# A new head and a new order for a fused attention and MLP kernel on one Trainium2 core

The kernel normalises 2048 rows, runs a sliding dilated attention and a GELU MLP on them, and adds both to the input. The change touches the first 20 us (what is loaded first, which engine takes which statistics, how the first chunk is projected) and then the order of everything after.

## The chip, the cores and the metric

One Trainium2 chip (trn2), one of its cores. The metric is the device time of one execution in microseconds, as a median of several runs; lower is better. The span in a profile (first to last instruction) is some 2.1 us shorter than the time of the same run. "Clock" is the granted clock of TensorE, 1.0 for full speed.

## The reference, cut to what matters

```python
# x: 1 x 2048 x 640 (bf16); 32 heads of 20; window W = 8, dilation 2; F = 1536
xn = layernorm(x)                                  # no gain, no bias
q, k, v = split_heads(xn @ wqkv)
# row s of head h looks at rows s, s-2, ..., s-14
attn = softmax(where(mask, q . k[s - 2*w], -1e9) * 20**-0.5)
A = (sum over w of attn[w] * v[s - 2*w]) @ wo
B = gelu(xn @ w1 + b1) @ w2 + b2
return x + A + B
```

## The kernel before

The rows are in 4 chunks of 512, each of 4 blocks of 128. Per chunk the rows are normalised, transposed, projected to q, k, v (TensorE), multiplied shifted against each other (VectorE), summed per head by TensorE into logits, turned into weights, spread over the head's 20 columns by four DMA issues of 256 KB (`ax`), multiplied with v (VectorE) and projected with `wo`, while TensorE and ScalarE run the MLP beside them.

The order on TensorE, VectorE, ScalarE and SyncE's queue is not written by hand. A planner at build time simulates the kernel: each piece has an engine, an estimated duration, a rank, needs, buffers and an earliest landing of its data. Whenever an engine is free, the ready piece of lowest rank comes next. The emitted order is then final; each engine takes its pieces strictly in this order. GpSimd has no order in the plan: it issues what it is given when its needs are met. Transfers too are entered with fixed durations or landing times.

Of the kernel before, what the change touches and what calls it, by code (L numbers as in the profile page):

```python
# [18 lines left out]
class Plan:  # L19
# [111 lines left out]
EPS = 1e-5  # L131
MASKED = -1e9
MW = 16
LASTB = S // P - 1
WARM = 44

GROUPS = (((0, 0, 4),), ((1, 0, 4),), ((0, 4, 5), (1, 4, 5)), ((2, 0, 4),), ((2, 4, 5),))
# [4 lines left out]
    "av1": 36.4, "av2": 74, "f12": 4.1, "f13": 69.4, "gj1": 19.4, "gj2": -19.4, "o02": -8.9, "o10": 15.3,  # L142
    "o12": -3.3, "o13": -11.3, "o20": 117, "o31": 57.5, "o33": 85.2, "ot0": 20, "pj22": -106.4, "pj31": -13.1,
    "qk1": -4.8, "qk2": 4.4, "st2": 164.2, "st3": 219.3, "xn0": -14.7,
# [3 lines left out]
def make_plan(fns, offsets=RANK):  # L148
# [10 lines left out]

    def done(n, which):  # L160
        if n:
            return [f"pc{n}{which}{to}" for to in range(KT)]
        return [f"gc{bl}{g}" for bl in range(BPC) for g, parts in enumerate(GROUPS) if which in [p[0] for p in parts]]

    pl.add("b1", VE, 0.1, -90, [], f("b1"), after=21.0)
    for n in range(NCH):
# [6 lines left out]
        for bl in range(BPC):  # L173
            land = (4.0, 4.0, 9.6, 9.6)[bl] if n == 0 else (0.0, 13.3, 17.1, 17.1)[n]
            r = -40 if n else -99
            pl.add(f"st{n}{bl}a", VE, 0.5, r, [], f("st", n, bl, 0), after=land)
            pl.add(f"st{n}{bl}", VE, 0.62, r, [f"st{n}{bl}a"] + ([f"rc{n}{bl - 1}"] if n == 0 and bl else []), f("st", n, bl, 1))
            if n == 0:
                pl.add(f"rs{n}{bl}", SE, 0.35, -99, [f"st{n}{bl}"], f("sqrt", n, bl, bl + 1), table="sqrt")
                pl.add(f"rc{n}{bl}", VE, 0.17, -99, [f"rs{n}{bl}"], f("rstd", n, bl, bl + 1))  # L180
# [3 lines left out]
        for bl in range(BPC):  # L184
            xn, tp = ("xn", n, bl), ("acc", "tp", n, bl)
            if n > 0:
                pl.add(f"xn{n}{bl}", SE, 0.81, early + -4.0, [f"rc{n}"], f("xn", n, bl), [xn])
                pl.add(f"tc{n}{bl}", DQ, 4.0 if n > 1 else 2.7, early - 3.0, [f"xn{n}{bl}"], f("td", n, bl), [xn, xnT], 21.5)
                continue

            for i, (a, b) in enumerate(((0, 2), (2, KT)) if bl == 0 else ((0, KT),)):
                u = "a" if b < KT else ""
                us = (b - a) / KT
                pl.add(f"xn{n}{bl}{u}", VE, 0.06 + 0.36 * us, -99, [f"rc{n}{bl}"], f("xn", n, bl, a, b), [xn])
                pl.add(f"tp{n}{bl}{u}", PE, (0.54 if bl == 0 else 0.3) * us, -99, [f"xn{n}{bl}{u}"], f("tp", n, bl, a, b), [xn, tp])
                pl.add(f"tc{n}{bl}{u}", SE, 0.16 + 0.49 * us, -99, [f"tp{n}{bl}{u}"], f("tc", n, bl, a, b), [tp, xnT])
        if n == 1:
            pl.add("ld", DQ, 9.2, -1000, [f"tc1{bl}" for bl in range(BPC)], f("ld"))
# [3 lines left out]
        if n == 0:  # L202
            for bl in range(BPC):
                for g, parts in enumerate(GROUPS):
                    ps, last = ("acc", "g", bl, g), max(p[0] for p in parts)
                    tos = sum(p[2] - p[1] for p in parts)
                    land = (6.4, 8.7, 11.8)[last]
                    r = -50 + (last == 2)
                    need, cut = [f"tc0{bl}"], 0
                    if bl == 0 and g == 0:  # L210
                        cut = 2
                        need.append(pl.add("ga00", PE, 0.112 * tos, r, ["tc00a"], f("gj", bl, g, 0, cut), [xnT, ps], land))
                    pl.add(f"gj{bl}{g}", PE, 0.056 * (KT - cut) * tos, r, need, f("gj", bl, g, cut, KT), [xnT, ps], land)
                    pl.add(f"gc{bl}{g}", SE, (0.27, 0.54, 0, 0.54)[tos - 1], -50, [f"gj{bl}{g}"], f("gc", bl, g), [ps] + [(q, k, v)[p[0]] for p in parts])
        for which, buf in enumerate((q, k, v)):
            for to in range(KT if n else 0):
                ps = ("acc", "p", n, which, to)
                r = early + (0 if which < 2 else 20.0)
                pl.add(f"pj{n}{which}{to}", PE, 1.08, r, [f"tc{n}{bl}" for bl in range(BPC)], f("pj", n, which, to), [xnT, ps])
                pl.add(f"pc{n}{which}{to}", SE, 0.52, early + 0.0, [f"pj{n}{which}{to}"], f("pc", n, which, to), [ps, buf])  # L220
            if which:
                need = done(n - 1, which) if n else []
                bufs = [buf] + ([("k" if which == 1 else "v", n - 1)] if n else [])
                pl.add(f"pad{n}{which}", SE, 0.26, early if n else -50, need, f("pad", n, which), bufs)
# [37 lines left out]
        for ft in range(FT):  # L262
            ps = ("acc", "h", n, ft)
            pl.add(f"f1{n}{ft}", PE, 1.08, base + 10.0 + 1.0 * ft, [f"tc{n}{bl}" for bl in range(BPC)], f("f1", n, ft), [xnT, ps], 22.5)
            pl.add(f"ge{n}{ft}", SE, 0.6, base + 0.0, [f"f1{n}{ft}", "b1"], f("ge", n, ft), [ps, hTs[ft]], table="gelu")
# [24 lines left out]
def kernel(  # L290
# [50 lines left out]
    nc.sync.dma_start(x_sb[:, 0, :], x_nb[:, 0, :])  # L341
    nc.scalar.dma_start(x_sb[:, 1, :], x_nb[:, 1, :])
    for s in range(3):
        nc.sync.dma_start(wqkv[s][:], wqkv_v[:, :, s * D : (s + 1) * D])
        if s == 1:
            nc.sync.dma_start(x_sb[:, 2:BPC, :], x_nb[:, 2:BPC, :])
    nc.sync.dma_start(b1_rt[0:FT, :], B_b1.rearrange("(t p) -> t p", p=P))
    for cs in (slice(BPC, 2 * BPC), slice(2 * BPC, NCH * BPC)):
        nc.sync.dma_start(x_sb[:, cs, :], x_nb[:, cs, :])
    nc.sync.dma_start_transpose(b1_t[:], b1_rt[:])  # L350
    nc.sync.dma_start(w1_sb[:], B_w1.rearrange("(t p) n -> p t n", p=P))
# [8 lines left out]
    zeros = consts.tile([P, P], BF16, name="zeros")  # L360
    nc.vector.memset(zeros[:], 0.0)  # L361
# [5 lines left out]
    nc.scalar.activation(warm[:], eps_t[:], ACT.Sqrt)  # L367
# [15 lines left out]
    std = consts.tile([P, NCH * BPC], F32, name="std")  # L383
    rstd = consts.tile([P, NCH * BPC], F32, name="rstd")
# [10 lines left out]
    def do_st(n, bl, i):  # L395
# [3 lines left out]
        if i:  # L399
            nc.vector.bn_aggr(mv[:, b, :], stats[:])  # L400

# [31 lines left out]
    def do_tp(n, bl, a, b):  # L433
        xn = tiles["xn", n, bl]
        tp = get(("tp", n, bl), lambda: psA.tile([P, 2 * CH], BF16, tag="acc", name="tp"))
        for t in range(a, b):
            nc.tensor.transpose(tp[:, t * P : (t + 1) * P], xn[:, t * P : (t + 1) * P], ident[:])  # L437

    def do_tc(n, bl, a, b):
        xnT = get(("xnT", n), lambda: xtp.tile([P, KT, CH], BF16, tag="xnT", name="xnT"))  # L440
        nc.scalar.copy(  # L441
            xnT[:, a:b, bl * P : (bl + 1) * P],
            tiles["tp", n, bl][:, a * P : b * P].rearrange("p (t m) -> p t m", t=b - a),
        )

    def do_td(n, bl):
        xnT = get(("xnT", n), lambda: xtp.tile([P, KT, CH], BF16, tag="xnT", name="xnT"))
        nc.sync.dma_start_transpose(xnT[:, :, bl * P : (bl + 1) * P], tiles["xn", n, bl][:])
# [43 lines left out]
    def do_gj(bl, g, a, b):  # L492
        cs = slice(bl * P, (bl + 1) * P)
        ps = get(("gps", bl, g), lambda: psA.tile([P, BPC, P], F32, tag="acc", name="gps"))
        slots = [(which, to) for which, lo, hi in GROUPS[g] for to in range(lo, hi)]
        pairs = [(i, ti) for i in range(len(slots)) for ti in range(a, b)]
        if b - a < KT:
            pairs.sort(key=lambda p: p[1])
        for i, ti in pairs:
            which, to = slots[i]  # L500
            nc.tensor.matmul(  # L501
                ps[:, i, :],
                lhsT=wqkv_p[which][:, ti, to, :],
                rhs=tiles["xnT", 0][:, ti, cs],
                start=(ti == 0 and (i == 0 or b == KT and a == 0)),
                stop=(ti == KT - 1 and (i == len(slots) - 1 or b == KT and a == 0)),
                skip_group_check=True,
            )

    def do_gc(bl, g):  # L510
        i = 0
        for which, a, b in GROUPS[g]:
            off = (0 if which == 0 else PAD) + bl * P
            nc.scalar.copy(qkv_tile(0, which)[:, a:b, off : off + P], tiles["gps", bl, g][:, i : i + b - a, :])
            i += b - a
# [205 lines left out]
    with tc.manual_schedule(engines=engines):  # L721

        idle = psL.tile([P, W, P], F32, tag="L", name="idle")
        for _ in range(WARM):
            nc.tensor.matmul(idle[:, 0, :], lhsT=zeros[:], rhs=zeros[:], start=True, stop=True)  # L725
# [32 lines left out]
```

## Time and profile before

| | before |
|---|---|
| time, median of 3 runs | 214.81 us (214.52 to 214.85) |
| span of the profiled run, clock | 212.4 us, 1.0 |
| busy: TensorE, VectorE, ScalarE | 97%, 82%, 52% |
| TensorE's first projection | 7.03 us |
| TensorE ends, span ends | 209.65, 212.4 us |

### The profile page before, as it was taken

The numbers are of one execution on the slowest core, as the hardware profiler recorded it, in microseconds if no ns is written. First come the engines' busy times: TensorE is split into PE (matmuls) and PEld (weight loads), VectorE is DVE, ScalarE is ACT, GpSimd is POOL, SyncE is SP. The second block draws the span as 40 slices with busy tenths as digits, with TensorE's granted clock in tenths as the row PEclk, the third lists the DMA queues.
The fourth block names the chain that finished last, engine by engine and source line by source line (L and its number), as shares of the span: only waits on it lengthen the run. The fifth ranks groups of instructions, "written<-read, shape, count | busy, mean of one in ns | idle before, by whom it ended". The sixth has DMA issues, their size and how long they took to land.

```text
span 212.4 us, 3961 instructions
## 1 busy us (share of the span) xinstructions
PE 206.9 (97%) x1670; PEld 121.7 (57%) x1693; DVE 174.4 (82%) x178; ACT 109.5 (52%) x193; POOL 19.7 (9%) x37
## 2 busy tenths in 40 slices
PE   8999999999999999999999999999999999999994
PEld 8799845655545555555555555455555455555552
DVE  3579999759999997599996999999999999972001
ACT  3568997798574654931353883503752511341120
POOL 2000000000020024101100010101110011101130
PEclk9999999999999999999999999999999999999999
DMA  6999528916829199993120027202114611122214
GB/s 216 365 362 376 93 50 275 322 24 132 206 64 163 37 287 196 197 195 89 15 30 0 0 31 200 31 3 31 14 21 48 180 19 22 27 29 31 34 16 76
DMA packets 23465, 23.95 MB, mean 113 GB/s; under 512 B 9112, under 2 KB 20632, under 8 KB 23448
## 3 DMA queue, kind: packets, MB, share of 16 engines
q1 hardware_dynamic: 17864, 16.49, 28.3%
q0 software_dynamic: 4144, 4.92, 17.2%
q10 hardware_dynamic: 1440, 2.29, 3.9%
q8 instruction: 13, 0.21, 0.4%
q14 instruction: 4, 0.03, 0.1%
HBM read 10.00 MB, written 7.54 MB: 83 GB/s over the span
## 4 chain that ended last, share of the span: by engine, by line
PE 97%; issue 1%; DVE 0%; ACT 0%
PE lo L684 27%; PE hps L653 24%; PE pps L484 23%; PE gps L501 8%; PE hi L686 8%; PE L L557 4%; PE idle L725 2%; PE tp L437 1%; ACT xnT L441 0%; DVE osb L714 0%; DVE zeros L361 0%
## 5 line engine op out<-in xcount | busy, mean ns | idle before, releaser
L653 PE MATMUL hps<-xnT,w_sb 128*128 128x512 bf16 x235 | 54.1, 379 | 0.3
L684 PE MATMUL lo<-w_sb,hT 128*128 128x512 bf16 x183 | 51.8, 379 | 0.0
L631 DVE TENSOR_TENSOR pv<-vT,ax 128x2560 bf16<-128x2560 bf16 x32 | 45.9, 1484 | 1.7 <-PE L L557 1.7
L535 DVE TENSOR_TENSOR prod<-qT,kT 128x2560 bf16<-128x2560 bf16 x32 | 45.4, 1484 | 0.0
L686 PE MATMUL hi<-w_sb,hT 128*128 128x128 bf16 x192 | 40.3, 219 | 0.6 <-issue 0.2
L664 ACT ACTIVATE hT<-hps,b1T 128x512 bf16<-128x512 f32 x48 | 31.6, 687 | 17.0 <-PE hps L653 13.3
L653 PEld LDWEIGHTS <-w_sb 128*128 128x128 bf16 x240 | 23.0, 98 | 26.7
L640 DVE TENSOR_TENSOR pv<-pv 128x5120 bf16<-128x5120 bf16 x12 | 33.9, 2825 | 0.4
L684 PEld LDWEIGHTS <-hT 128*128 128x128 bf16 x192 | 18.7, 98 | 22.8 <-issue 0.6
L691 ACT CAST osb<-lo 128x512 bf16<-128x512 f32 x15 | 8.8, 585 | 44.0 <-issue 28.0
L697 POOL DMA_DIRECT2D out_dram<-osb x15 | 12.9, 863 | 110.5 <-ACT osb L692 110.5
L684 PE MATMUL lo<-wo,oT 128*128 128x512 bf16 x79 | 23.0, 379 | 0.0
L686 PEld LDWEIGHTS <-hT 128*128 128x128 bf16 x192 | 18.4, 98 | 1.5
L398 DVE BATCH_NORM_STATS2 stats<-x_sb 128x6 f32<-128x320 bf16 x32 | 14.0, 469 | 5.1 <-DMA x_sb<-in_A_x_dram 5.1
L484 PE MATMUL pps<-xnT,wq_sb 128*128 128x512 bf16 x71 | 16.9, 380 | 0.2
L484 PE MATMUL pps<-xnT,wv_sb 128*128 128x512 bf16 x73 | 16.9, 379 | 0.1
L686 PE MATMUL hi<-wo,oT 128*128 128x128 bf16 x80 | 16.9, 219 | 0.1
L484 PE MATMUL pps<-xnT,wk_sb 128*128 128x512 bf16 x73 | 16.8, 379 | 0.1
L705 DVE TENSOR_TENSOR osb<-lo,x_sb 128x512 bf16<-128x512 f32 x1 | 0.7, 692 | 16.1 <-PE lo L684 16.1
L520 ACT CAST qT<-pps 128x512 bf16<-128x512 f32 x15 | 8.8, 585 | 9.2 <-PE pps L484 9.2
L684 PEld LDWEIGHTS <-oT 128*128 128x128 bf16 x80 | 7.8, 98 | 9.4
L484 PEld LDWEIGHTS <-wk_sb 128*128 128x128 bf16 x75 | 8.7, 118 | 7.3 <-issue 0.2
(62 smaller groups left out, 205.9 us busy)
## 6 DMA issues: line engine op xcount, KB each, us to landing
w_sb<-in_B_w_dram SPq DMA_DIRECT2D x2, 1920.0 KB, 9.2
out_dram<-osb POOLq DMA_DIRECT2D x15, 160.0 KB, 3.4
ax<-attn SPq DMA_DIRECT2D x8, 256.0 KB, 5.4
ax<-attn ACTq DMA_DIRECT2D x8, 256.0 KB, 5.6
out_dram<-x_sb SPq DMA_DIRECT2D x3, 640.0 KB, 4.3
out_dram<-b2bc POOLq DMA_DIRECT2D x3, 640.0 KB, 8.2
x_sb<-in_A_x_dram SPq DMA_DIRECT2D x1, 1280.0 KB, 13.3
wq_sb<-in_A_wqkv_dram SPq DMA_DIRECT2D x1, 800.0 KB, 4.8
```

The costliest lines, as they stand in the source:

```text
L398: nc.vector.bn_stats(stats[:, i, :], x_sb[:, b, i * (D // 2) : (i + 1) * (D // 2)])
L484: nc.tensor.matmul(ps[:], lhsT=wqkv_p[which][:, ti, to, :], rhs=xnT[:, ti, :], start=(ti == 0), stop=(ti == KT - 1),)
L501: nc.tensor.matmul(ps[:, i, :], lhsT=wqkv_p[which][:, ti, to, :], rhs=tiles["xnT", 0][:, ti, cs], start=(ti == 0 and (i == 0 or b == KT an ...
L520: nc.scalar.copy(dest[:, to, off : off + CH], tiles["pps", n, which, to][:])
L535: nc.vector.tensor_tensor(out=prod[:, i, :, :], in0=qkv_tile(n, 0)[:], in1=qkv_tile(n, 1)[:, :, off : off + CH], op=ALU.mult,)
L631: nc.vector.tensor_tensor(out=pv[:, i, :, :].rearrange("p t (j c) -> p t j c", j=BPC), in0=qkv_tile(n, 2)[:, :, off : off + CH].rearrange( ...
L640: nc.vector.tensor_tensor(out=ta[:], in0=ta[:], in1=tb[:], op=ALU.add)
L653: nc.tensor.matmul(ps[:], lhsT=w1_sb[:, ti, ft * P : (ft + 1) * P], rhs=tiles["xnT", n][:, ti, :], start=(ti == 0), stop=(ti == KT - 1),)
L664: nc.scalar.activation(hT[:], tiles["hps", n, ft][:], ACT.Gelu_apprx_tanh, bias=b1T[:, ft : ft + 1], scale=1.0)
L684: nc.tensor.matmul(lo[:], lhsT=lhs, rhs=rhs[:, 0:CH], start=first, stop=last)
L686: nc.tensor.matmul(hi[:, 0 : D - CH], lhsT=lhs, rhs=rhs[:, CH:D], start=first, stop=last)
L697: nc.gpsimd.dma_start(rows, tiles["osb", n, bl][:], accum_op=ALU.add)
```

## The change

Its intent: TensorE is the bound, and it idles only in the head, so bring useful work forward there and save some matmuls' overhead. Block 0 is loaded first and alone, q's weights come in two parts, block 2 and block 3 apart. Block 0's transposes get PSUM tiles of their own, so that the first copy needn't wait for all five. Block 1's mean and variance are taken by ScalarE from accumulated sums. k and v of chunk 0, and q of its blocks 2 and 3, are projected for two blocks at a time. The new plan has other ranks and landing times, hence another order everywhere.

```diff
-WARM = 44
+WARM = 40
 RANK = {
-    "av1": 36.4, "av2": 74, "f12": 4.1, "f13": 69.4, ...
+    "ad02": 84.2, "av1": 114.8, "f11": 43.4, "f12": 139.3, "f13": 100, ...
-            land = (4.0, 4.0, 9.6, 9.6)[bl] if n == 0 else (0.0, 13.3, 17.1, 17.1)[n]
+            land = (3.1, 3.6, 6.1, 8.7)[bl] if n == 0 else (0.0, 12.9, 21.8, 21.8)[n]
+                pl.add("sm", SE, 0.75, -99, [], f("sum1"), after=land)      # block 1 on ScalarE
...                                                          # nm, me, sq likewise
-    nc.sync.dma_start(x_sb[:, 0, :], x_nb[:, 0, :])
-    nc.scalar.dma_start(x_sb[:, 1, :], x_nb[:, 1, :])
-    for s in range(3): ...                                  # q, k, blocks 2 and 3, v
+    load_x(0, 1)
+    load_x(1, 2)                                            # now SyncE's queue
+    load_w(0, 0, 2)
+    load_w(0, 2, KT)
+    load_x(2, 3)
+    load_w(1)
+    load_x(3, BPC)
+    load_w(2)
...
+    load_x(BPC, 2 * BPC)
+    for c in range(2): ...                                  # w1 in two halves
+    load_x(2 * BPC, NCH * BPC)                              # chunks 2 and 3 now behind w1
+    def do_sum1():
+        nc.scalar.activation(trash()[:], x_sb[:, 1, :], ACT.Identity, accum_out=acc1[:])
...
+        pool, tag = (psO, own) if own else (psA, "acc")     # own PSUM tiles for block 0
+        tp = pool.tile([P, 2 * CH], BF16, tag=tag, name="tp")
...
+    def do_gp(which, pair, a, b):                           # 256 columns: two blocks
+                nc.tensor.matmul(ps[:, to - a, :], lhsT=wqkv_p[which][:, ti, to, :],
+                    rhs=tiles["xnT", 0][:, ti, pair * 2 * P : (pair + 1) * 2 * P], ...)
```

## The prediction

> **What bounds the kernel now.** I read four views in this order: the page's busy table with its chain that ended last, the waits of TensorE, the timeline of the first 9 us, and TensorE's timeline afterwards. From the page:
>
> ```profile
> PE 206.9 (97%) x1670; PEld 121.7 (57%) x1693; DVE 174.4 (82%) x178; ACT 109.5 (52%) x193; POOL 19.7 (9%) x37
> PE 97%; issue 1%; DVE 0%; ACT 0%
> ```
>
> TensorE is busy for 97% of the span and carries 97% of the chain that ended last. VectorE, at 82%, is second and is not on the chain. The 97% includes warm-up, so I ask what TensorE waited for. The waits, TensorE only:
>
> ```profile
> PE idle L725 <- DVE zeros L361: 1.0, 1, 1.0
> PE gps L501 <- ACT xnT L441: 0.5, 1, 0.5
> PE hi L686 <- issue: 0.2, 1, 0.2
> ```
>
> There are only two named waits in the whole run, both in the first 7.03 us. Everything this change can win must come from there, or from the matmuls themselves. The timeline of the head (start, duration, engine and operation):
>
> ```profile
> 0.99 4.87 PE L725 MATMUL idle<-zeros 128*128 128x128 bf16 x44 [0.99 <-DVE zeros L361]
> ...
> 3.71 0.89 DVE L398 BATCH_NORM_STATS2 stats<-x_sb 128x6 f32<-128x320 bf16 x2 [2.77 <-DMA x_sb<-in_A_x_dram]
> ...
> 4.87 0.30 ACT L404 ACTIVATE std<-mv,eps_t 128x1 f32<-128x1 f32 x1 [2.18 <-DVE mv L400]
> 5.20 0.16 DVE L408 RECIPROCAL rstd<-std 128x1 f32<-128x1 f32 x1
> 5.40 0.63 DVE L424 TENSOR_SCALAR xn<-x_sb,mv,rstd 128x256 bf16<-128x256 bf16 x2
> ...
> 5.80 0.77 PE L437 MATMUL tp<-ident,xn 128*128 128x128 bf16 x5
> ...
> 6.61 0.75 ACT L441 COPY xnT<-tp 128x256 bf16<-128x256 bf16 x2 [1.44 <-PE tp L437]
> ...
> 7.03 1.28 PE L501 MATMUL gps<-xnT,wq_sb 128*128 128x128 bf16 x20 [0.46 <-ACT xnT L441]
> ```
>
> 44 matmuls that only warm the array fill the time until the first block of x is there. The first useful projection begins at 7.03. The copy of transposed parts 0 and 1 begins only at 6.61, after all five transposes: both halves share a PSUM tile. TensorE's rates afterwards:
>
> ```profile
> 8.74 4.00 PE gps L501 x70
> 16.37 8.65 PE gps L501 x155
> 25.30 8.37 PE hps L653 x38
> ```
>
> These are lines of the chain. 128-column matmuls come every 55.8 ns (8.65/155), and 512-column ones every 0.216 us (eight tiles of five take 8.64 us from 24.86 to 33.50). A pair of 512 and 128 columns takes 0.272 us (12 pairs in 3.26 us).
>
> **A tally from 7.03.** Projection of chunk 0: 300 x 0.0558 = 16.7. Transposes of blocks 1 to 3: 15 x 0.0558 = 0.8. First layer of the MLP: 240 x 0.216 = 51.8. Projections of chunks 1 to 3: 225 x 0.216 = 48.6. Logits: 2.30 + 6 x 1.21 = 9.6. Outputs: 272 x 0.272 = 73.9. Sum 201.5. The final matmul's stream ends about 209.5 (end at 209.65, less the 0.16 by which one modelled matmul exceeds its spacing). So 209.5 - 7.03 = 202.5, and all later stalls together are about 1.0 us. The total time (214.81) is 2.4 us more than the span (212.4).
>
> **What the Trainium skill says.**
> 1. "TensorE: Matmul & The Clock Gate", section "Back-to-back issue gap": an isolated gap of N/2.4 + 2.5 ns when warm, and about 81 ns at N = 128 in a stream that also loads weights. The trace agrees with the first (55.8 ns and 216 ns) and not with the 81 ns.
> 2. The same page, section "Part 1: The HAM clock gate": the array starts at half rate and is released after about 3.4 us of activity, in a free-running window. The trace agrees: 44 warm-up matmuls in about 4.7 us (107 ns each), and 55.8 ns from 7.03.
> 3. "DMA: Bandwidth & Descriptors", section "Anatomy of one DMA": about 2.0 us fixed plus bytes/436e3. For 160 KB alone that is 2.4 us. The trace has 2.9 and 3.1 us for the two blocks sent together: compatible.
> 4. "PSUM — Partial Sum Buffer", section "Engine vs sequencer instructions": the queues of ScalarE and VectorE are strictly first in, first out, and matmuls start in program order. So one late input holds back all behind it. In the trace ScalarE's idle 1.44 us before 6.61 fits that.
>
> **The change part by part.**
>
> *Block 0 first.* In the trace both blocks were issued at 0.74/0.75, block 0 in 2.9 us (landing about 3.65). Alone at first, it saves the half of 320 KB that is not its own: 160 KB at 365 GB/s (page, GB/s row) is 0.45 us. I expect landing near 3.25, block 1 near 3.7.
>
> *Block 1's statistics on ScalarE.* It adds two passes over 640 columns (normalising that shape costs 0.935 us in the trace) and one small one (0.30). VectorE loses two BN_STATS (0.44 each) and one aggregate (0.21), which were behind block 0 anyway. But the sum of block 1 stands before block 0's square root on ScalarE: 3.7 + 0.93 = 4.63, whereas block 0's statistics are ready at 3.25 + 1.13 = 4.38 (3.71 to 4.84 before). So the root starts 4.63 instead of 4.87: of 0.45 us won by loading, 0.24 is left.
>
> *Own PSUM tiles, copy on VectorE.* Normalising starts 0.24 earlier, at 5.16; the second half ends 5.79; the first two transposes, 0.4 us after normalising starts, end about 5.95; VectorE then copies (0.37, taken from the ScalarE row) until 6.35. First projection at about 6.4 instead of 7.03: 0.6 us.
>
> *The rest of the head.* ScalarE: small pass to 5.2, squares to 6.1, root to 6.4, copy of parts 2 to 4 to 6.9. TensorE: 10 matmuls from 6.4, 5 more at 6.95, block 1's transposes about 7.25, 10 more to 8.1, block 1's 25 to about 9.5, first k tiles (10 of 256 columns) to 10.6. The built order then has block 2's transposes, whose square root group stands behind **block 3's statistics** on VectorE. Block 3 lands after the same 2.3 MB as blocks 2 and 3 now (9.54), say 9.3. Statistics 1.13, reciprocal and normalising about 0.5: transposes at 10.95, a stall of about 0.3. Useful work before it: 50 x 0.0558 + 5 x 0.0558 + 10 x 0.1092 = 4.16, so TensorE is as if it had run without a gap from 10.95 - 4.16 = 6.8. Against 7.03: **0.25 us**. If block 3 lands at 8.7, as the changed plan assumes, TensorE itself is the limit, the effective start is about 6.4, and this is 0.6.
>
> *Block pairs.* 250 matmuls of 128 columns become 125 of 256. Interpolating the two rates, 256 columns take 55.8 + 128 x (216 - 55.8)/384 = 109.2 ns. Saved: 125 x (111.6 - 109.2) = **0.3 us**. Fewer ScalarE copies are off the path.
>
> *Warm-up on the constant of ones, 40.* Starts about 0.25 earlier, ends near 5.05; the transposes come near 5.55. Off the path.
>
> *New order.* q and k of chunk 0 are ready about 19.7 instead of 23, since most of v is put off; VectorE starts its products 3 us earlier. I walked VectorE's and TensorE's new order with the durations above: the logit pieces of TensorE at 79.5, 95.3, 110.9 find products ready at 77.5, 94.0, 109.5. No new stall, but only 1.3 to 2 us to spare. Old stalls of 1.0 us may fall by a few tenths.
>
> Sum: 0.25 to 0.6, plus 0.3, plus 0 to 0.3: 0.55 to 1.2, taken as **0.9 us**: 213.9.
>
> **Rivals.**
> (a) *The saved head is taken by the next landing.* TensorE waits for block 3 or for k and v weights: bytes before them are the same as now (k and v landed 8.6 and 11.7). For: DMA is full (365 GB/s) until 20 us. Against: transposes are placed between other work. Then 214.3 to 214.8.
> (b) *VectorE becomes the bound in the middle.* For: margins of 1.3 us in a hand walk; all residual and bias writes now stand in the queue ahead of the first spread of attention weights, and could delay it. Against: its start 3 us earlier. It would cost 0.5 to 2 us: 214.5 to 216.
> (c) *Cold clock.* Fewer warm-up matmuls and small gaps near 5 to 6.4 us leave the array at half rate longer: 51 ns for each of perhaps 15 to 50 matmuls, 0.8 to 2.5 us. Against: before too had gaps of 0.4 us and was warm at 7.03.
> (d) *All goes as the plan wants*: 1.2 to 1.5 us, 213.3 to 213.6.
>
> **Range and chances.** (d) and the main line carry most: 213.1 to 214.9 should hold it 8 times in 10. A gain of 2% (4.3 us) is impossible from a head in which useful work starts at 7.03 and data at 3.7; a loss of 2% needs (b) or (c) at their worst.
>
> **What would show it.** First projection near 6.4 and, on the chain, no stall over 0.5 us after block 2's transposes; pair matmuls 109 ns apart; the first products of VectorE near 20; TensorE's waits after 11 us still under 1 us. It is wrong if block 0 lands no earlier, if ScalarE's sum does not delay the root, if early projections run at 107 ns, or if TensorE waits for logits' products after 70 us.

## More of the kernel before

```python
for name, n in (("acc", 4), ..., ("osb", 2), ("xn", 2), ...):   # buffers
    pl.pool(name, n)
...
for bl in range(BPC):       # chunks 1 to 3: ScalarE normalises, a DMA transposes
    pl.add(f"xn{n}{bl}", SE, 0.81, early - 4.0, [f"rc{n}"], f("xn", n, bl), [xn])
    pl.add(f"tc{n}{bl}", DQ, 4.0 if n > 1 else 2.7, early - 3.0, [f"xn{n}{bl}"], ...)
pl.add(f"xp{n}", DQ, 0.3, base + 30, ["ld"], f("xp", n))    # x to the output
pl.add(f"xb{n}", DQ, 0.0, base + 33, [f"xp{n}"], f("xb", n))
...
def do_xp(n):               # a plain write of 4 blocks of x into the output (SyncE's queue)
    nc.sync.dma_start(dst, x_sb[:, cs, :])
def do_xb(n):               # bias b2 added onto it, an accumulating DMA (GpSimd)
    nc.gpsimd.dma_start(dst, b2bc[:].unsqueeze(1).to_broadcast(...), accum_op=ALU.add)
...
# the loads in their order
nc.sync.dma_start(x_sb[:, 0, :], x_nb[:, 0, :])
nc.scalar.dma_start(x_sb[:, 1, :], x_nb[:, 1, :])       # ScalarE's queue
for s in range(3):                                      # q, k, v weights
    nc.sync.dma_start(wqkv[s][:], wqkv_v[:, :, s * D : (s + 1) * D])
    if s == 1:
        nc.sync.dma_start(x_sb[:, 2:BPC, :], x_nb[:, 2:BPC, :])
... # b1, chunk 1 of x, chunks 2 and 3 of x, w1
for _ in range(WARM):                                   # 44 matmuls on zeros, to warm TensorE
    nc.tensor.matmul(idle[:, 0, :], lhsT=zeros[:], rhs=zeros[:], start=True, stop=True)
for t in make_plan(fns).run():
    t["fn"]()
```

The later text uses the planner's names: `tp` and `tc` are transposes and their copies (`tc20` to `tc23`: the DMA transposes of chunk 2), `xn` normalises, `xp` and `xb` are the writes above, `o` and `oc` are the output products and ScalarE's copies of them.

GpSimd's bias adds in the kernel before:

```profile
60.97 1.44 POOL L465 DMA_DIRECT2D out_dram<-b2bc  x1 [58.92 <-DMA out_dram<-x_sb]
78.41 1.29 POOL L465 DMA_DIRECT2D out_dram<-b2bc  x1 [16.00 <-DMA out_dram<-x_sb]
...
```

Chunk 2's first transposes are issued at 36.21. Only one write of x and its add come before chunk 3's transposes (61.64), and three after. The transposes and the adds hardly meet.

What the prediction did not show is how SyncE's queue goes from 30 to 80 us. The timeline of that queue in the kernel before (start, length of the group of issues, source line, operation, out<-in, count):

```profile
36.21 2.63 SPq L452 DMA_TRANSPOSE xnT<-xn  x2
...
56.08 0.58 SPq L461 DMA_DIRECT2D out_dram<-x_sb  x1
61.64 12.95 SPq L452 DMA_TRANSPOSE xnT<-xn  x4
74.64 2.29 SPq L461 DMA_DIRECT2D out_dram<-x_sb  x3
```

## The result, and the profile after

The changed kernel took **235.13 us** (median of 4 runs, 232.79 to 237.16; the last of these is slow for its distance to the fastest), against 214.83 us (214.52 to 215.21) for the kernel before on the same chip. The ratio is 1.092, interval 1.085 to 1.098: slower. A ratio here is the mean time of one kernel's runs over that of the other's in the same rounds, so not quite the ratio of the medians. Executions over 1.5% slower than the fastest of the same kernel are left out of the means.

From the page of the changed kernel, whose span is 232.2 us, the busy times and the clock in 40 slices of 5.8 us:

```profile
PE 209.6 (90%) x1564; PEld 121.1 (52%) x1564; DVE 174.8 (75%) x177; ACT 112.4 (48%) x192; POOL 19.7 (8%) x37
...
PEclk9999999999995699999999999999999999999997
```

TensorE is busy 90% instead of 97%, and the clock falls to half in one stretch. The waits of TensorE (source line, waited for, us in total, times, longest):

```profile
PE hps L729 <- ACT hT L740: 9.7, 1, 9.7
PE lo L760 <- DVE oT L722: 1.8, 1, 1.8
PE tp L493 <- DVE xn L478: 1.2, 2, 0.8
PE idle L802 <- PEq L819: 0.8, 1, 0.8
PE gps L581 <- DMA wk_sb<-in_A_wqkv_dram: 0.7, 1, 0.7
PE gps L550 <- DMA wq_sb<-in_A_wqkv_dram: 0.5, 1, 0.5
```

One wait of 9.7 us is half of the loss: TensorE stood before a tile of the MLP (`hps`) until ScalarE's GELU freed a PSUM tile. The stretch lies at 66 to 76 us, so I followed it through the other engines. SyncE's queue, timeline:

```profile
33.98 7.22 SPq L514 DMA_DIRECT2D out_dram<-x_sb  x4
46.91 1.63 SPq L691 DMA_DIRECT2D ax<-attn  x2
53.47 37.80 SPq L505 DMA_TRANSPOSE xnT<-xn  x8
```

GpSimd, timeline:

```profile
46.08 5.46 POOL L518 DMA_DIRECT2D out_dram<-b2bc  x4 [44.04 <-DMA out_dram<-x_sb]
```

All four writes of x now stand at 34 us, and so GpSimd issues all four accumulating bias adds at 46 to 51.5 us. Chunk 2's transposes, which went out at 36.21 before, go out at 53.47, behind those adds, because the new order also normalises chunk 2 later (first block at 52.53 instead of 35.26). The transfers from 44 to 70 us (KB each, median us from issue to landing), first the kernel before, then the changed one:

```profile
out_dram<-b2bc POOLq DMA_DIRECT2D x1, 640.0 KB, 8.2
xnT<-xn SPq DMA_TRANSPOSE x5, 4.5
```

```profile
out_dram<-b2bc POOLq DMA_DIRECT2D x3, 640.0 KB, 19.8
...
xnT<-xn SPq DMA_TRANSPOSE x2, 15.9
```

A transpose that landed in 4.5 us (median) takes 15.9. ScalarE, timeline:

```profile
69.19 0.92 ACT L474 ACTIVATE xn<-x_sb,nmr,rstd 128x640 bf16<-128x640 bf16 x1 [11.06 <-DMA xnT<-xn]
73.01 0.92 ACT L474 ACTIVATE xn<-x_sb,nmr,rstd 128x640 bf16<-128x640 bf16 x1 [2.90 <-DMA xnT<-xn]
...
75.24 1.84 ACT L740 ACTIVATE hT<-hps,b1T 128x512 bf16<-128x512 f32 x3
```

ScalarE has two buffers for normalised rows. At 58 us it came to the third block of chunk 2, whose buffer was still being read by a transpose, and stood 11.06 us, then 2.90 us more. The GELUs of chunk 1 stand behind these in its queue, though their inputs were ready. Without GELUs the four PSUM tiles filled, and TensorE stopped. Its timeline after the wait:

```profile
75.98 6.15 PE L729 MATMUL hps<-xnT,w_sb 128*128 128x512 bf16 x20 [9.65 <-ACT hT L740]
```

The next product starts at 81.97, so these twenty matmuls of 512 columns hold TensorE for 6.0 us; at full rate it is 4.3 (20 x 0.216). That is another 1.7 us: the clock is 0.50 from 70 to 79 us, in and after the idle stretch.

The head, timeline of the changed kernel (views of all engines and of TensorE):

```profile
3.05 0.89 DVE L437 BATCH_NORM_STATS2 stats<-x_sb 128x6 f32<-128x320 bf16 x2 [3.05 <-DMA x_sb<-in_A_x_dram]
...
5.87 0.72 PE L550 MATMUL gps<-xnT,wq_sb 128*128 128x128 bf16 x10
...
7.05 0.47 PE L550 MATMUL gps<-xnT,wq_sb 128*128 128x128 bf16 x5 [0.47 <-DMA wq_sb<-in_A_wqkv_dram]
```

```profile
10.47 1.29 PE L581 MATMUL gps<-xnT,wk_sb 128*128 128x256 bf16 x10 [0.70 <-DMA wk_sb<-in_A_wqkv_dram]
12.59 0.45 PE L493 MATMUL tp<-ident,xn 128*128 128x128 bf16 x5 [0.84 <-DVE xn L478]
```

Block 0 lands at 3.05 (before 3.71) and the first projection starts at 5.87 (before 7.03), but then three waits follow (0.47, 0.70 and 0.84 us), each for a load that now lands later than before. Block 2's transposes start at 12.59 with 4.16 us of useful work before them, so TensorE is as if it had started at 8.43 without a gap; less the 0.3 us that pairs save, the head is 1.1 us worse than the 7.03 of before.

The end, timeline of the changed kernel:

```profile
226.26 0.59 ACT L767 CAST osb<-lo 128x512 bf16<-128x512 f32 x1 [3.54 <-DMA out_dram<-osb]
...
227.31 0.86 POOL L773 DMA_DIRECT2D out_dram<-osb  x1 [3.44 <-ACT osb L768]
```

TensorE ends at 224.2, but ScalarE's last copy waits 3.54 us for one of two output buffers, and the last output block is issued at 227.31. From TensorE's end to the span's end it is 8.0 us; before it was 2.7, since the last accumulating output went out at 206.09, ahead of TensorE's end.

**Tally.** Wait for GELU 9.7, half clock after it 1.7, head 1.1, wait for the attention's output (`oT`) 1.8, tail 8.0 - 2.7 = 5.3: together 19.6 us, for 19.8 us of span. These are readings of two traces. The experiments test the causes.

### The profile page after: what moved, and what is told of

Its sections match the earlier page's. It is cut to its first block, busy times and chain, and to the rows that moved or that the text cites. A ratio compares the mean times of both kernels' runs of the same rounds, so it can differ in the third digit from the quotient of the medians.

```text
span 232.2 us, 3724 instructions
## 1 busy us (share of the span) xinstructions
PE 209.6 (90%) x1564; PEld 121.1 (52%) x1564; DVE 174.8 (75%) x177; ACT 112.4 (48%) x192; POOL 19.7 (8%) x37
## 4 chain that ended last, share of the span: by engine, by line
PE 47%; issue 33%; DMA 10%; POOL 4%; ACT 2%; SPq 1%; DVE 1%; POOLq 0%
PE pps L537 21%; PE hps L729 11%; DMA xnT<-xn 7%; PE lo L760 6%; PE gps L581 5%; POOL out_dram L773 4%; DMA x_sb<-in_A_x_dram 3%; PE L L633 3%; PE hi L762 1%; ACT hT L740 1%; SPq L374 1%; SPq L371 1%; ACT L740 1%; DVE stats L437 0%; POOLq L830 0%
## 5 line engine op out<-in xcount | busy, mean ns | idle before, releaser
L729 PE MATMUL hps<-xnT,w_sb 128*128 128x512 bf16 x240 | 55.9, 387 | 9.7 <-ACT hT L740 9.7
L707 DVE TENSOR_TENSOR pv<-vT,ax 128x2560 bf16<-128x2560 bf16 x32 | 45.8, 1486 | 12.1 <-DMA ax<-attn 11.2
L760 PE MATMUL lo<-w_sb,hT 128*128 128x512 bf16 x192 | 53.4, 379 | 0.0
L437 DVE BATCH_NORM_STATS2 stats<-x_sb 128x6 f32<-128x320 bf16 x30 | 13.0, 468 | 8.2 <-DMA x_sb<-in_A_x_dram 8.2
L474 ACT ACTIVATE xn<-x_sb,nmr,rstd 128x640 bf16<-128x640 bf16 x12 | 11.1, 923 | 14.0 <-DMA xnT<-xn 14.0
L537 PEld LDWEIGHTS <-wv_sb 128*128 128x128 bf16 x75 | 8.7, 118 | 7.4 <-issue 0.2
## 6 DMA issues: line engine op xcount, KB each, us to landing
out_dram<-b2bc POOLq DMA_DIRECT2D x3, 640.0 KB, 19.8
```

The costliest lines, as they stand in the source:

```text
L437: nc.vector.bn_stats(stats[:, i, :], x_sb[:, b, i * (D // 2) : (i + 1) * (D // 2)])
L474: nc.scalar.activation(xn[:], x_sb[:, i, :], ACT.Identity, bias=nmr[:, i : i + 1], scale=rstd[:, i : i + 1])
L537: nc.tensor.matmul(ps[:], lhsT=wqkv_p[which][:, ti, to, :], rhs=xnT[:, ti, :], start=(ti == 0), stop=(ti == KT - 1),)
L707: nc.vector.tensor_tensor(out=pv[:, i, :, :].rearrange("p t (j c) -> p t j c", j=BPC), in0=qkv_tile(n, 2)[:, :, off : off + CH].rearrange( ...
L729: nc.tensor.matmul(ps[:], lhsT=w1_sb[:, ti, ft * P : (ft + 1) * P], rhs=tiles["xnT", n][:, ti, :], start=(ti == 0), stop=(ti == KT - 1),)
L760: nc.tensor.matmul(lo[:], lhsT=lhs, rhs=rhs[:, 0:CH], start=first, stop=last)
```

## The experiments

Each kernel gave correct results. "Ratio" is against the kernel before in the same rounds, with a 95% interval. Edits are to the changed kernel unless said. `move(names, after)` moves pieces in the planned order, which is otherwise kept.

### 1. Are the writes the cause of the middle stall?

**e1_writes_later**: all writes of x and bias adds behind chunk 2's transposes.

```diff
+        move(("xp0", "xb0", "xp1", "xb1", "xp2", "xb2", "xp3", "xb3"), "tc23")
```

> The changed kernel with one move in the order of issue: the four residual writes and the four bias adds stand behind the transposes of chunk 2 instead of ahead of them. All engines keep their order otherwise. Theory A (the transposes of chunk 2 wait for DMA engines that the writes and bias adds fill): transposes land in 3 to 5 us instead of 16, TensorE's 9.7 us wait for the first GELU of chunk 1 falls under 1 us, the clock stays at 1.00, and the time falls from 235 to 221-225 us. Theory B (the transposes are late because chunk 2 was normalised late, at 52 us instead of 36): the wait stays, time above 231 us.

Measured 227.96 us (226.39 to 230.02), ratio 1.056 (1.050 to 1.063), span 224.4. The 9.7 us wait is gone. The gain is 7 us instead of 11, because the stall moved: TensorE's waits in this run now have

```profile
PE pps L537 <- ACT kT L596: 1.9, 1, 1.9
PE pps L537 <- ACT qT L596: 1.7, 1, 1.7
```

The adds now lie in front of chunk 3's transposes, which take 11.4 us to land. Waits for k and q 3.6, `oT` 1.6, tail 5.3 more than before, head 1.0: 11.5 of the remaining 12.0 us of span.

**e2_bias_later** meant to move the bias adds alone.

```diff
+        move(("xb0", "xb1", "xb2", "xb3"), "tc23")
```

> Only the four bias adds (accumulating DMAs from GpSimd's queue) are moved behind the transposes of chunk 2; the four plain residual writes stay ahead. Theory A1 (the accumulating adds, 20 us each to landing, are what fills the DMA engines): as with both moved, 221-225 us, transposes land in 3 to 6 us. Theory A2 (2.4 MB of plain writes ahead in the same queue hold the transposes): time stays above 231 us, landing above 12 us.

Measured 234.64 us (232.93 to 235.65), ratio 1.089. A failed experiment: GpSimd is not in the fixed order, so its adds were still issued at 45.49 us, and the wait stayed at 9.7. It tells nothing about the adds.

**e8_bias_held** does what e2 could not: the bias row is loaded only behind chunk 2's transposes, so the adds can't start earlier, while the writes of x stay where they are.

```diff
     def do_ld():
-        nc.sync.dma_start(b2bc[:], b2_bcast)
+        # moved: issued after "tc23"
```

> Repeats the question that the run with bias adds moved in order failed to ask, as GpSimd has nothing else to do and issued them at 45 us all the same: the row of biases is loaded behind the transposes of chunk 2, so the adds cannot begin before that, while the plain residual writes stay ahead. Theory A1 (the accumulating adds fill the DMA engines): chunk 2's transposes land in 3 to 6 us, TensorE's 9.7 us wait goes below 1 us, time 221-229 us (chunk 3's transposes may now meet the adds). Theory A2 (the plain writes ahead in the queue do it): wait stays above 7 us, time above 231 us.

Measured 230.28 us (229.41 to 231.35), ratio 1.072 (1.068 to 1.076). Chunk 2's stall is gone while the plain writes stand where they stood. Its transposes, issued at 53.53, land as fast as any (median of the transfers from 53 to 63 us):

```profile
xnT<-xn SPq DMA_TRANSPOSE x4, 2.6
```

So the accumulating adds are what delays the transposes. The adds, issued at 66.1 now, meet chunk 3's transposes, and a new wait for k of 3.5 us and one for q of 1.2 us appear.

**e3_in_place** tests the other half of the chain, ScalarE's buffers: chunk 2 is normalised in place in `x_sb`, so ScalarE never waits for a transpose. Transposes and adds stay as they are. (The residual of chunk 2 has been written by then.)

```diff
+        if n == 2:
+            xn = x_sb[:, i, :]
+            tiles["xn", n, bl] = xn
+        else:
             xn = get(("xn", n, bl), lambda: lnp.tile(...))
```

> Writes and adds stay where the change put them; chunk 2 is normalised in place in x's own tile, so its four blocks no longer share two buffers and the third normalising on ScalarE need not wait for the first transpose to land. Theory A (TensorE starves because ScalarE, in order, is held at that normalising with the GELUs of chunk 1 behind it): GELUs start near 59 us, TensorE goes on until it needs chunk 2's transposed x near 70 us, its wait falls from 9.7 to 0-4 us, time 222-228 us, although the transposes still land late (10 us or more). Rival (only the landing counts, not the buffers): TensorE's wait stays at 8 us or more, time above 231 us.

Measured 227.66 us (224.90 to 231.05), ratio 1.053 (1.046 to 1.061). The transposes still take up to 14.8 us, but TensorE waits for them only

```profile
PE pps L541 <- DMA xnT<-x_sb: 2.3, 1, 2.3
```

So the slow transposes cost 2.3 us by themselves; the 9.7 arose because ScalarE stood behind its two buffers with ready GELUs behind it.

### 2. The tail

**e4_tail** moved the five pieces of the last block's products, and the early half of its output, back behind the other blocks.

```diff
+        move(("o330", "o331", "o332", "o333", "o334", "oclo"), "o314")
```

> Only the end of TensorE's order is put back as before: the last block's pieces (written by VectorE and a plain DMA) run last instead of ahead of blocks 13 and 14. Theory T (the changed order ends with a block whose result goes through ScalarE, one of two output buffers and an accumulating DMA, 8.0 us from TensorE's end to the end of the span against 2.7 before): tail back to 2.5-4 us, time 230-232 us. Rival (the tail is long because everything ran late): tail stays near 8 us, time 234-236 us.

Measured 236.59 us (235.59 to 237.71), ratio 1.100: a miss. The tail fell from 8.0 to 4.9 us, not to the expected 2.5 to 4. The final block still took its output buffer ahead of the copy that comes last, and the moved products had been filling the wait for `oT`, which grew from 1.8 to 4.2 us.

**t1_tail_last** moved all of the last block, its second half too, to the very end, as in the kernel before.

```diff
+        move(("o330", "o331", "o332", "o333", "o334", "oclo", "ohi", "ochi"), "od31")
```

> The changed kernel, only the end of the order as before, this time with the last block's output tile taken after those of the other blocks (the first try took it before them and so kept the lack of buffers). Theory T (two buffers, and a last block that leaves by an accumulating DMA, make the 8.0 us): last accumulating DMA is issued 3 us or more before TensorE ends, TensorE's end to span's end 2.5-3.5 us; but the wait for the attention sums (1.8 us) grows to about 4 us as in the first try, so the time is 230.5 to 233 us. Rival: tail above 5 us again.

Measured 235.17 us (233.76 to 236.17), ratio 1.094 (1.089 to 1.099). The tail became 3.2 us (TensorE ends at 230.75, the span at 233.9), as before the change. But TensorE ends 6.5 us later than in the changed kernel: the wait for `oT` is again 4.2 us, and after it matmuls of 512 columns last 0.63 us instead of 0.38 for 5 us. The tail and the late attention hang together: what the plan had put in front of `oT` was filler, and taking it away costs what the tail gives back.

**e7_three_out** gives the output a third buffer.

```diff
-    outp = ctx.enter_context(tc.tile_pool(name="outp", bufs=2))
+    outp = ctx.enter_context(tc.tile_pool(name="outp", bufs=3))
```

> The changed kernel with three output buffers instead of two, all orders kept. In the changed kernel the last copy on ScalarE waited 3.5 us for an accumulating DMA to free its buffer, and the span ended 8.0 us after TensorE's last matmul. Theory (buffers: the last block's tile now takes one of two while the others alternate on the other): the 3.5 us wait is gone, TensorE's end to span's end falls to 4.0-5.5 us, time 231.5 to 232.5. Rival (accumulating DMAs are served one after the other anyway): tail stays at 7 us or more, time 234-236.

Measured 231.66 us (231.01 to 234.78), ratio 1.077 (1.075 to 1.079). The wait of 3.5 us is gone and the last accumulating output goes out at 224.04. Of the tail 5.7 us are left, so the third buffer alone takes away 2.3 of the 5.3 us lost there. The old order of the last block alone (t1, with two buffers) took away 4.8, so the two repairs overlap, and only the buffer came without a loss elsewhere.

### 3. Everything repaired at once, and the order as a whole

**e6_all** combined the repairs: chunk 0's writes behind `tc23`, the others behind `tc33`, the first six loads as before, three output buffers.

```diff
+        move(("xp0", "xb0"), "tc23")
+        move(("xp1", "xb1", "xp2", "xb2", "xp3", "xb3"), "tc33")
```

> Three mends together: the writes and adds of chunk 0 behind the transposes of chunk 2 and those of chunks 1 to 3 behind the transposes of chunk 3, the first loads as before, three output buffers. If the three losses named (9.7 + 1.8 us in the middle, 1.1 us in the head, 5.3 us at the end) are the whole of the 19.8 us, the span is within 3 us of before: time 213.5 to 218 us. If above 220 us, a fourth cause is missing (chunk 2 normalised 16 us later than before, or the margins of the attention order).

Measured 223.37 us (222.11 to 223.96), ratio 1.039 (1.035 to 1.043), against 213.5 to 218 expected: the list of causes was not complete. Left in the trace are the waits for `oT` (2.0), for an output copy (1.0) and for logits (0.4), 1.1 us in the head and 2.9 us more tail than before: 7.4 of 7.8 us. Behind `oT` stands VectorE. In the changed kernel its products with the last chunk's attention weights wait 8.21 us for the spread (`ax`) at 193.17; in e6 8.4 us. The kernel before placed products of another chunk into this gap.

**h1_order_kept** puts the question the other way round: all new parts of the head and the first eight loads stay, and from chunk 1 on the old order is emitted (with the old order of the later loads, and all of chunk 0's v projected before the MLP as in the kernel before).

```diff
-        for t in make_plan(fns).run():
-            t["fn"]()
+        by = {t["name"]: t for t in make_plan(fns).run()}
+        order = """pad01 pad02 st00a st00 sm rs00 me nm rc00 xn00a ...""".split()
+        for name in order:
+            by[name]["fn"]()
```

> All parts of the changed head (block 0 first, own PSUM tiles, block 1's statistics on ScalarE, pairs, the first eight loads), but from chunk 1 on the order of all engines as before, all of v projected before the MLP, and the later loads as before (all of x ahead of the MLP weights). Theory O (the new order, not the parts, costs the time): middle, attention and tail as before, only the head's own balance of about +1.1 us against before (start of unbroken work 1.4 us later, pairs 0.3 us saved): time 214.5 to 216.5 us. Rival (a part of the head does the damage later, for example through what its loads delay): above 219 us.

Measured 215.93 us (215.69 to 215.99), ratio 1.0047 (1.0032 to 1.0062), span 213.6. **The order after the head, with the later loads that belong to it, costs 19 of the 20 us. The head's own parts cost 1.0 us.** Ranks and later loads were not told apart.

### 4. Why the head gains nothing

The prediction had the head 0.55 to 1.2 us faster, and it was slower.

**e5_loads** put the first six loads back (block 1 on ScalarE's queue, q whole, blocks 2 and 3 together) in the changed kernel.

```diff
     load_x(0, 1)
-    load_x(1, 2)
-    load_w(0, 0, 2)
-    load_w(0, 2, KT)
-    load_x(2, 3)
+    nc.scalar.dma_start(x_sb[:, 1, :], x_nb[:, 1, :])
+    load_w(0)
     load_w(1)
-    load_x(3, BPC)
+    load_x(2, BPC)
     load_w(2)
```

> The changed kernel with the first six loads as before (block 1 of x on ScalarE's queue, the q weights in one piece, blocks 2 and 3 of x together), nothing else. The changed kernel began its first MLP matmul at 21.35 us; by the prediction's count it should have been about 19.7. Theory L (eight small loads one behind the other feed the DMA engines too slowly, so q, k weights and block 3 land 1 to 1.9 us later than before): q weights land by 6.1, k by 8.8, block 3 by 9.7, first MLP matmul at 19.6 to 20.2 us, time 1.2 to 1.8 us lower (232.8 to 234.2). Rival (ScalarE's statistics and the order of the head cost it): first MLP matmul stays near 21.3 us.

Measured 236.72 us (235.84 to 238.28), ratio 1.100. The waits for q and k were gone as expected, but VectorE, in its fixed order, took block 2's statistics (which wait for the load) ahead of the copy of block 1's transposes, and ScalarE's copy behind it waited 3.5 us. The 11.0 us stall in the middle covers the rest, so this base is poor for questions of 1 us. The runs below start from h1.

**h2_q_whole** is h1 with q's weights in one load.

```diff
-    load_w(0, 0, 2)
-    load_w(0, 2, KT)
+    load_w(0)
```

> As the run with the order kept, but q's weights in one load instead of two: the k and v weights and block 3 are issued one issue (0.5 us) earlier. Theory L (issue of small loads one behind the other starves the DMA engines, 128 to 300 GB/s between 3 and 7.5 us against 325 to 390 before): k lands about 0.5 us earlier, block 3 too, the transposes of block 2 start at 12.1 instead of 12.6, time 0.3 to 0.6 us below the run with the order kept. Rival: no difference beyond 0.2 us.

Measured 217.78 us (217.28 to 218.24), ratio 1.013 (1.011 to 1.016): 1.9 us slower than h1. The theory that splitting q was the fault fell. q landed at 7.8 us, TensorE waited 1.8 us for it, and then the 50 q products and five transposes took 5.7 us (7.80 to 13.5) instead of some 3.1: half rate (55 pieces at about 104 ns; at full rate 55.8).

**b1_before_two** is the kernel *before* with two edits: block 1 of x on SyncE's queue, and own PSUM tiles for block 0.

```diff
-    nc.scalar.dma_start(x_sb[:, 1, :], x_nb[:, 1, :])
+    nc.sync.dma_start(x_sb[:, 1, :], x_nb[:, 1, :])
-        tp = get(("tp", n, bl), lambda: psA.tile([P, 2 * CH], BF16, tag="acc", name="tp"))
+        own = "lo" if (bl, a) == (0, 0) else "hi"
+        pool, tag = (psO, own) if bl == 0 else (psA, "acc")
+        tp = pool.tile([P, 2 * CH], BF16, tag=tag, name="tp")
```

> The kernel before with only two ideas of the change: block 1 of x is issued behind block 0 on the same queue, and block 0's two groups of transposes have PSUM tiles of their own (both still copied by ScalarE). Theory: block 0 lands at 3.05-3.2 instead of 3.7, the first copy need not wait for all five transposes (0.4 us), the first projection starts at 6.1-6.4 instead of 7.03, nothing later moves, time 0.4 to 0.9 us below before (ratio 0.996 to 0.998). Rival (the k and v weights, 0.4 us later, or VectorE in order take it back): no gain beyond 0.1 us.

Measured 216.40 us (215.10 to 217.22), ratio 1.0065 (1.0026 to 1.0105): no gain. Block 0 landed at 3.17, but q at 8.2, two us later than before, and TensorE waited 2.4 us for it.

**v3_own_tiles** is b1 without the move of block 1's load: the PSUM tiles alone.

> The kernel before with block 0's two sets of transposes in PSUM tiles of their own and nothing else (b1_before_two, 216.4 us, had this and block 1 on SyncE's queue). Theory Q: b1's loss was all due to the queue; here q lands at about 6.0, the first copy starts at 6.1 to 6.3 instead of 6.6, the first projection at 6.6 to 6.8 instead of 7.03, and the time is 214.3 to 214.8. Rival: the tiles of their own cost (pool psO is wanted elsewhere): over 215.3.

Measured 214.71 us (214.30 to 216.20), ratio 0.9992 (0.9959 to 1.0025). The six runs fall into two groups, 214.3 to 214.7 and 215.9 to 216.2. The profiled one is of the slower group: q landed at 7.4 although the loads are those of before, the clock was 0.50 from 7.5 to 10.5 us, and block 2's transposes start 1.65 us later than in the kernel before (14.23 against 12.58), enough for its 1.5 us. The rival (the tiles cost) is not supported by the first group; the theory's number is met only there.

**v1_x1_other_queue** is h1 with block 1 on ScalarE's queue again.

```diff
-    load_x(1, 2)
+    nc.scalar.dma_start(x_sb[:, 1, :], x_nb[:, 1, :])
```

> h1_order_kept (all of the changed head, the old order from chunk 1 on: 215.9 us) with one edit: block 1 of x is issued from ScalarE's queue again instead of behind block 0 on SyncE's. Theory Q: the late landing of q, k and block 3 comes from this one move; the two runs that have block 1 on ScalarE's queue keep 229 to 387 GB/s from 2 to 5 us, the four that have it on SyncE's fall to 59 to 113 GB/s at about 3.3 us. Then the dip is gone, the wait for q's second part (0.3) and for k (0.7) are gone, block 0 lands at about 3.7 instead of 3.0, the first projection starts at 6.5 to 6.8 and the time is 213.9 to 214.7, just below the kernel before. Rival S: the dip comes from issuing small loads one by one (q in two, block 2 alone); then the dip stays, k still makes PE wait 0.5 or more, and the time is 215.4 to 216.2.

Measured 215.51 us (214.87 to 216.16), ratio 1.0007 (0.9978 to 1.0036), where h1 had 1.0047. The dip of the transfer rate at 3.1 to 4 us went, but another came at 5.6, q's second part was still 0.55 us late, and the clock was 0.50 from 8 to 11 us; but the profiled run is the slowest of the six. In all nineteen traces the lowest quarter of a microsecond between 3 and 4 us has 41 to 118 GB/s where block 1 is on SyncE's queue (eleven traces), and 287 or more where it is on ScalarE's (eight). On one queue the weights of q are also issued later, at 1.67 instead of 1.20 us. That the queue makes this dip is well supported; that it alone makes the loss is not: inconclusive.

**v2_loads_as_before** is h1 with all of the first six loads as before, and VectorE's order mended: block 2's statistics behind the copy of block 1's transposes.

```diff
-rc01 ga tc00b xn01 st02a gb2 tp01 gb3 tc01a tc01b gb4 ...
+rc01 ga tc00b xn01 gb2 tp01 gb3 tc01a tc01b st02a gb4 ...
```

> h1_order_kept with the first six loads as in the kernel before (block 1 on ScalarE's queue, q whole, blocks 2 and 3 in one load) and, for VectorE, block 2's first statistics moved behind the copy of block 1's transposes, which in e5_loads waited 3.5 us behind them. If the head's own parts (own PSUM tiles, sums on ScalarE, block pairs) are worth what the prediction said (0.25 to 0.6 us) once the loads land as before: first projection at 6.7 to 6.9, no wait of PE over 0.5 up to 12 us, 214.0 to 214.7. Rival: they are worth nothing or less even then (a wait for block 2's or 3's transposes appears at 11 to 13 us): 214.9 to 216.

Measured 214.94 us (214.61 to 215.60), ratio 0.9989 (0.9964 to 1.0014): the 1.0 us is gone, but no gain. TensorE's timeline shows why:

```profile
5.94 0.79 PE L489 MATMUL tp<-ident,xn 128*128 128x128 bf16 x5 [0.74 <-DVE xn L474]
6.72 1.76 PE L546 MATMUL gps<-xnT,wq_sb 128*128 128x128 bf16 x15
```

The warm-up matmuls end at 5.20, and for 0.74 us nothing runs. The next 15 products take from 6.72 to 8.27, when the following transposes start, or 103 ns each; at full rate it is 55.8. The traces of e5 and e6, with 40 warm-up matmuls and gaps of 0.67 and 0.66 us, show the same (105 and 103 ns).

**w1_warm48** is v2 with 48 warm-up matmuls instead of 40, which nearly reach the transposes (the gap is 0.26 us).

```diff
-        for _ in range(WARM):
+        for _ in range(48):
```

> v2_loads_as_before (214.94 us, the same as before) with 48 warm-up matmuls in place of 40. Theory C: with the old loads the changed head starts its transposes at 5.94, while 40 warm-up matmuls end at 5.20; in this gap of 0.7 us the array falls back to half rate, and in v2's trace the matmuls of the projection start some 110 ns apart for 128 columns from 6.7 to about 9.3, which costs about 1 us. With 48 the warm-up reaches the transposes, the first 15 projection matmuls take about 0.9 to 1.2 us instead of 1.76, and the time is 213.9 to 214.5. Rival N: the half rate has nothing to do with the gap[...]: the rate in the trace and the time stay as in v2, 214.7 to 215.2.

Measured 214.82 us (214.74 to 215.61), ratio 0.9979 (0.9934 to 1.0025). The timeline of TensorE:

```profile
6.70 1.00 PE L546 MATMUL gps<-xnT,wq_sb 128*128 128x128 bf16 x15
...
12.11 0.45 PE L489 MATMUL tp<-ident,xn 128*128 128x128 bf16 x5 [1.09 <-DVE xn L474]
```

Half right: the rate is full from 6.70 (15 products in 0.83 us, to the transposes at 7.53), and the first k products start at 9.76 instead of 11.08. The 1.3 us then turn into a wait of 1.09 us for block 2, which stands in the order ahead of k products that are ready. In both runs block 2's transposes start at 12.1, set by the landing of blocks 2 and 3 at 9.4 and VectorE's statistics behind it.

**w2_k_ahead** puts ten of those k products ahead of block 2's transposes, and two q copies ahead of block 2's square root on ScalarE.

```diff
-rs02 st03 hj100 gc4 rc02 rs03 xn02 gc1 rc03 tp02 xn03 hc100 hj101 ...
+gc4 gc1 rs02 st03 hj100 rc02 rs03 xn02 rc03 hj101 tp02 xn03 hc100 ...
```

> w1_warm48 (214.82 us; its saved 1.3 us of half rate turned into a wait of 1.09 us for block 2's normalised rows at 12.1) with ten more k products of blocks 0 and 1 placed ahead of block 2's transposes, and two q copies ahead of block 2's square root on ScalarE so that their PSUM tiles are free. Theory D: the head is bound by the landing of blocks 2 and 3 (9.4 us) and what stands in the order at that moment; the wait at 12.1 goes, work that is ready fills it, and the time is 213.7 to 214.3, below both kernels. Rival: the products only push the wait elsewhere (a PSUM tile not free, or v's weights, at 11 to 15 us); PE still waits 0.8 us or more in all up to 16 us and the time stays at 214.6 to 215.1.

Measured **214.22 us** (214.04 to 215.16), ratio 0.9961 (0.9940 to 0.9982), span 211.8: faster than both kernels, by 0.4% of the kernel before. The interval leaves out 1. Its waits in the head, beside the warm-up's start, are

```profile
PE gps L546 <- DVE xnT L494: 0.2, 1, 0.2
PE tp L489 <- DVE xn L474: 0.2, 1, 0.2
```

So the changed head's own tiles, ScalarE sums and block pairs, with the old loads, 48 warm-up matmuls and an order mended by hand, gain 0.85 us in the medians, about what the prediction worked out for the head. In the traces the first product of the MLP starts at 24.30 instead of 24.86. No run separates the parts, and none gives the kernel before the longer warm-up alone, so how the 0.85 divides is not shown.

## Why the prediction was right or wrong

The prediction said 213.9 us, 213.1 to 214.9 in 8 cases of 10, and it was 235.1. Its ceiling on the gain held; what failed is the other side.

**Right.** Block 0 landed earlier (3.05; 3.25 predicted) and the first projection started earlier (5.87; 6.4). One reason for the earlier start is that the sum of block 1 took 0.74 us, not 0.93, so block 0's root began at 4.28, not 4.63. Pairs run 109 ns apart, as interpolated. Warm-up was enough in the changed kernel: the early products ran at full rate (rival (c) did not come there). The worth of the head's parts, 0.55 to 1.2 us, agrees with what w2 got (0.85), but w2 needed repairs that the prediction did not foresee, so the agreement is partly luck. (The prediction's 2.4 us between time and span takes the two from different runs; run by run it is about 2.1. This drops out of the difference.)

**Wrong, in the order of cost.**

1. *"No new stall, but only 1.3 to 2 us to spare."* This step walked VectorE and TensorE and left ScalarE and SyncE's queue out. The stall of 9.7 us plus 1.7 us of cold clock came by them. Rival (b) had seen that "all residual and bias writes now stand in the queue", but named only the first spread of attention weights as their victim, and 0.5 to 2 us. That spread was late too (up to 12.8 us to land instead of at most 6.3, and VectorE waited 2.57 us for it), but TensorE's stall came through chunk 2's transposes. e8 shows that the adds delay them, e3 that the two buffers on ScalarE turn a wait of 2.3 us into 9.7.
2. *The tail* is no step of the prediction at all: "all later stalls together are about 1.0 us" was read off the kernel before and kept. It cost 5.3 us. e7 shows that a third output buffer takes away 2.3 of it; t1 that the old order of the last block takes away 4.8, but only by moving the loss in front of the tail.
3. *VectorE's walk.* Its first products were to start "near 20", 3 us earlier; they started at 22.10 instead of 23.02, 0.9 us earlier. The logits, which the prediction feared, still made TensorE wait for none. The walk went wrong at the end: the spread of the last chunk's attention weights kept VectorE waiting 8.2 us, with nothing to fill the gap, and that is behind the wait for `oT`, 1.8 us. The prediction states no figure for a spread, so how the walk missed it stays open.
4. *The landing of block 3 and k.* Block 3 was to land at 9.3, "after the same 2.3 MB" as before, and k with the same bytes before it as before, when it landed at 8.6; they landed at 10.9 and 10.4, because the bytes did not flow at the same rate. Rival (a) named this turn (time saved in the head is taken by the next landing) but bounded it at zero gain; it was a loss of 1.1 us.
5. *The chances.* A loss of 2% was to need "(b) or (c) at their worst". A change that reorders every engine's list should not have been bounded so tightly, when only two of four lists had been walked.

**Still open.** Ranks against later loads as the source of the new order's cost; the reason for the dip on one queue, and why q's landing differs by more than a microsecond between runs with the same loads (v3); the spread of the changed kernel's own runs, 232.8 to 237.2.

## What to carry to other kernels

When a change gives a new static order, walk *every* in-order engine and every queue, and for each long DMA ask which small transfer behind it feeds a two-buffer pool, and what useful work stands behind that pool on its engine. Time saved in a head shows only when no later wait takes it back: here it had to pass the clock, a landing and one misplaced piece before 0.85 us came through. Look also for ready work that fills the wait for a late input before moving it: in t1 moving it cost what the tail gave back.

## What the Trainium skill lacked or had wrong

- "DMA: Bandwidth & Descriptors", section "Anatomy of one DMA": its 2.0 us plus bytes/436e3 gives 3.5 us for 640 KB (an estimate by that page). An accumulating bias add of 640 KB took 8.2 us in the kernel before, with no other add in flight, and 19.8 us (median) in the changed kernel, where four were issued within 5.5 us and the spreads of attention weights beside them. The section has no figure for accumulating transfers.
- The same page, section "Issuing engines are not separate DMA queues": it says that transfers of all issuers interleave on the same engines. The trace agrees: SyncE's transposes took 15.9 us behind GpSimd's adds and 2.6 in e8, where the adds came later. It says that issuing from several engines saves only sequencer time. Here, with block 1 of x on the same queue as block 0, the rate fell to 118 GB/s or less between 3 and 4 us in eleven traces, and in none of eight with two queues. The later issue of q (1.67 instead of 1.20 us) may be that sequencer time, so the page is not shown wrong; what it lacks is that half a microsecond of it can matter so early.
- "TensorE: Matmul & The Clock Gate", section "Part 1: The HAM clock gate": it gives about 3.4 us for an idle window (a later section of the page has short idle times make the clock swing, without a length). Shorter gaps went with the half rate here. In v3 the clock was 0.50 from 7.5 to 10.5 us after two gaps of 0.8 and 1.05 us with work between them, and in v2 a gap of 0.74 us at the end of the warm-up went with the half rate (103 ns for 128 columns) to about 9.5 us; with 48 warm-up matmuls and a gap of 0.26 us (w1) the rate was full at 6.7. In v2's stretch the recorded clock said 1.00, so the rate has to be read from the starts of the matmuls.
- No page that I found gives what accumulating a sum costs on ScalarE: the pass over 128x640 took 0.74 us, and reading the sum is an instruction of its own, of 0.19 us.
